# Late Q pairs evacuated two PSUM banks at a time, five of them behind the kv sum: one change to a hand-ordered attention and MLP kernel

## The chip, the cores and the metric

The kernel runs on one core of one Trainium2 chip, in one launch. The metric is the device time of that launch in microseconds; the time before is the median of three runs. A core has TensorE (PE, matmuls), VectorE (DVE), ScalarE (ACT), GpSimd (POOL) and SyncE (SP), here used to issue DMAs. Matmuls write PSUM, eight banks of 512 fp32 values in each of 128 partitions; ACT and DVE read them out ("evacuate").

## The reference

One token block of S = 2048 tokens and D = 448 goes through a linear-attention layer and a gated MLP, each behind a LayerNorm and with a residual:

```python
h  = x + A(layernorm(x))
h2 = h + B(layernorm(h))

def A(x):                                    # 16 heads of 28
    q, k, v = split(x @ wqkv)
    phi = lambda t: where(t > 0, t + 1, exp(t)) + 1e-6
    kv  = sum over s of phi(k)[s, d] * v[s, e]      # per head
    z   = sum over s of phi(k)
    o   = (phi(q) @ kv) / (phi(q) @ z + 1e-6)
    return o @ wo

def B(x):                                    # 448 -> 1792 -> 448
    return (gelu(x @ w_gate) * (x @ w_up)) @ w_down
```

All inputs and the output are bf16. The sum kv over all 2048 tokens has to be complete before any o can be formed.

## The kernel before, in words

Tokens are cut into 16 tiles of 128. Each step is a named task on one engine. A task graph (`_Graph`) derives the waits from the buffers that a task reads and writes, PSUM banks among them; the sequence on each engine is not found at run time but written out, as five strings in `ORDERS` (PE, ACT, DVE, POOL, SP). An engine runs its string strictly in order, so a task that waits holds all that stand behind it on that engine.

Names, with a tile number t, a group number q or a task number v behind them:

- Front LayerNorm, for each tile: bnst, bnag (DVE, statistics, L467 and L468), ln, rstd (ACT), negm (POOL), norm (DVE for the first four tiles, L491, else POOL, L492). Tiles 0 to 3 are transposed on TensorE (tr, L500) and copied out by ev: ev0 and ev1 on DVE (L530), ev2 and ev3 on ACT (L532). Tiles 4 to 15 get a small copy dup (ACT, L534) and a DMA transpose xT, issued on SP.
- K and V, for each tile (`kv_tile`): k and v (PE) are two halves that write the same two banks, one for K and one for V; ek = exp of K (ACT, L570), cl = clamp (POOL, L571), ph = phi(K) in SBUF (DVE, L573), evv = V to SBUF (ACT, L575). Four small accumulations in two tasks, acc..a and acc..b, add phi(K)^T V to banks 6 and 7.
- Q (`q_pair`): four token chunks of 512 with two pairs each, so eight pairs n = 2c + h, in tasks qa and qb (qa00, qb00 to qa31, qb31); a pair fills two banks with two groups of 112 rows. Pairs 0 to 3 lie between the K and V tiles (`EVENTS`), pairs 4 to 7 behind them. For pairs 0 to 3 each group is evacuated by eq (exp, L618), cq (clamp on POOL, L619) and pq (max and add on DVE straight from PSUM, L620). For pairs 4 to 7 (`SPLIT`) it is eq (exp into its final place, L626), rq (a plain copy of q into the free buffer `xn`, L627), cq (clamp in place on POOL, L628) and pq (max and add on DVE, all operands in SBUF, L629), so that both PSUM reads are ACT's.
- Behind the kv sum: kz1, kz2 (DVE, masks of the sum), then for tiles 0 and 1 nd (numerator and denominator, PE), rd and om (reciprocal and product on DVE, L656 and L657), tro (transpose, PE), evo (ACT), wo (PE), hr (residual, DVE, L662), hbnst and hbnag, hln and hrstd (ACT), normh and wrap (DVE), trh (transpose, PE), evh (copy: evh0 on ACT, evh1 on DVE). Later tiles go in pairs: nd..a and nd..b, a DMA transpose oT, wo..a and wo..b, then the second LayerNorm on POOL and a DMA transpose hT.
- MLP: gu (gate and up, PE), ge (gelu, ACT, L832), hm (product, DVE, L834), down (PE), out (residual, DVE, L758). gu0 to gu6 cover tiles 0 and 1. Task v uses gate bank `BK_G[v % 2]` and up bank `BK_U[v % 2]`.

Two halves of a product (qa and qb, k and v, acc..a and acc..b, nd..a and nd..b, wo..a and wo..b) use the two 64-row halves of TensorE on two banks crosswise: what the upper rows write in the first half, the lower rows write in the second. The graph therefore makes the second half wait for the end of the first. The tables `KV_BANKS` and `Q_BANKS` say which two of the banks 0 to 5 a tile or a pair uses, and with that which evacuation it waits for.

The two tasks nd0 and nd1, tro, trh, most of wo0 and wo1, and the last down tasks use all 128 rows of TensorE; all else uses 64.

Of the kernel before, what the change touches and what calls it, by code (L numbers as in the profile page):

```python
# [7 lines left out]
ALU = mybir.AluOpType  # L8
# [206 lines left out]
def _c_act(n):  # L215
    return 0.05 + n / 1200.0


def _c_dve(n, rate=1.0):
# [6 lines left out]
    ("q", 2), ("kv", 10), ("kv", 11), ("kv", 12), ("q", 3), ("kv", 13), ("kv", 14), ("kv", 15),  # L226
)
KV_BANKS = ((3, 2), (4, 5), (2, 0), (1, 3), (0, 2), (3, 1), (5, 4), (1, 3), (4, 5), (2, 0), (5, 4), (0, 2), (3, 1), (2, 0), (1, 3), (4, 5))
Q_BANKS = ((5, 4), (2, 0), (3, 1), (4, 5), (0, 1), (2, 3), (0, 1), (2, 3))


def bass_sequential_preLN__linear_attn_block__glu_gated_geglu__prompt_kernel(
# [16 lines left out]
    STAT_GROUPS = [[0], [1], [2], [3]] + [[t, t + 1] for t in range(4, T, 2)]  # L249
    N_DVE_NORM = cfg.get("n_dve_norm", 4)  # L250
# [6 lines left out]
    SPLIT = cfg.get("split", (4, 5, 6, 7))  # L257
# [3 lines left out]
    with es:  # L261
# [81 lines left out]
        def bank(*b):  # L343
            return [b_ps[x] for x in b]
# [4 lines left out]
        BK_G, BK_U = (0, 1), (6, 7)  # L349
# [19 lines left out]
        def op(eng, fn, r, w, name, dur, key=None, after=()):  # L369
            if key is None:  # L370
                ik[0] += 0.01
                key = ik[0]
            return G.add(eng, fn, r=r, w=w, name=name, dur=dur, key=key, after=after)
# [134 lines left out]
        first = []  # L508

        for ts in STAT_GROUPS:  # L510
            kln = 1.0 + 1.4 * ts[0] - (30.0 if ts[0] < 2 else 0.0)
            for t in ts:
                first.append(ln_stats(t, x_sb[:, t, :], b_x[t], st1, mv1, b_st1, b_mv1, kln, after=first[-1:] if t < 3 else ()))
# [3 lines left out]
            for t in ts:  # L517
                dve = t < N_DVE_NORM
                nrm = op("dve" if dve else "pool", norm(t, xn[:, t, 0:D], x_sb, mv1, rs1, None if dve else nm1), [b_x[t], b_mv1[t], b_rs1[t]] + ([] if dve else [b_nm1[t]]), [b_xn[t]], "norm%d" % t, 0.31 if dve else 0.69, kln)
                if t == 1:  # L520
                    first.append(nrm)
                tok = slice(t * 128, (t + 1) * 128)
                ktr = 4.0 + 1.6 * t
                if t < N_PE_TR:
# [4 lines left out]
                    if t < 2:  # L529
                        op("dve", lambda e, xv_=xv_, tv=tv: e.tensor_copy(xv_, tv), bank(*pb), [b_xnT[t]], "ev%d" % t, 0.33, ktr)  # L530
                    else:
                        op("act", lambda e, xv_=xv_, tv=tv: e.activation(xv_, tv, AF.Identity), bank(*pb), [b_xnT[t]], "ev%d" % t, _c_act(512), ktr)  # L532
# [382 lines left out]
```

## Time and profile before

| what | us |
|---|---|
| median of three runs (198.08 to 198.22) | 198.17 |
| profiled execution | 197.88 |
| its span, first to last instruction | 196.1 |
| TensorE busy | 191.2 |
| VectorE busy | 118.8 |
| ScalarE busy | 76.7 |
| GpSimd busy | 49.1 |

Times in the rows are microseconds from the start of the span. A timeline row has start, length, engine, line, operation, output<-inputs, shape and count; in brackets stands the idle time just before it and what ended it. Matmuls are pipelined: their rows overlap, so that TensorE's pace is read from the distance of two starts. In a row of a group, the number behind the bar is busy time, then the mean ns of one instruction, then the idle time before and its releasers. Many matmuls share the line of a helper (L435) and are told apart by their tiles and shapes: wkv_sb is K and V, wq_sb is Q, v,pk the accumulation, kvz,pqT nd, wo_sb wo, wgu_sb gu, wd_sb down.

### The profile page before, as it was taken

The numbers are of one execution on the slowest core, as the hardware profiler recorded it, in microseconds if no ns is written. First come the engines' busy times: TensorE is split into PE (matmuls) and PEld (weight loads), VectorE is DVE, ScalarE is ACT, GpSimd is POOL, SyncE is SP. The second block draws the span as 40 slices with busy tenths as digits, with TensorE's granted clock in tenths as the row PEclk, the third lists the DMA queues.
The fourth block names the chain that finished last, engine by engine and source line by source line (L and its number), as shares of the span: only waits on it lengthen the run. The fifth ranks groups of instructions, "written<-read, shape, count | busy, mean of one in ns | idle before, by whom it ended". The sixth has DMA issues, their size and how long they took to land.

```text
span 196.1 us, 5375 instructions
## 1 busy us (share of the span) xinstructions
PE 191.2 (98%) x2192; PEld 131.1 (67%) x2192; DVE 118.8 (61%) x303; ACT 76.7 (39%) x211; POOL 49.1 (25%) x100
## 2 busy tenths in 40 slices
PE   7999999999999999999999999999999999999994
PEld 7555557654489774975555656788887666679554
DVE  3999746548899974952975870972665544241512
ACT  3489865766884210330342440241234444211100
POOL 4089964533332060400220310130310000000000
PEclk9999999999999999999999999999999999999999
DMA  6985656992764318043142035134060000010111
GB/s 193 376 252 97 83 103 168 241 241 55 139 233 89 62 30 142 28 92 61 47 96 54 2 76 74 36 67 94 3 129 14 3 0 0 3 47 3 47 47 47
DMA packets 37256, 17.53 MB, mean 89 GB/s; under 512 B 28272, under 2 KB 36336, under 8 KB 37232
## 3 DMA queue, kind: packets, MB, share of 16 engines
q1 hardware_dynamic: 36352, 16.45, 36.6%
q10 hardware_dynamic: 880, 0.75, 1.2%
q8 instruction: 17, 0.28, 0.6%
q14 instruction: 7, 0.06, 0.1%
HBM read 8.72 MB, written 1.84 MB: 54 GB/s over the span
## 4 chain that ended last, share of the span: by engine, by line
PE 87%; DVE 7%; DMA 4%; issue 1%; ACT 0%; SPq 0%; DVEq 0%
PE ps L435 80%; PE ps L782 5%; DMA oT<-o_sb 2%; DVE st L467 2%; DMA x_sb<-in_A_x_dram 2%; DVE o_sb L657 1%; DVE xn L491 1%; DVE x_sb L662 1%; DVE hh L834 0%; DVE rd L656 0%; DVE hn L491 0%; DVE mv L468 0%; DVE xnT L530 0%; DVE pqT L629 0%; PE ps L674 0%
## 5 line engine op out<-in xcount | busy, mean ns | idle before, releaser
L435 PE MATMUL ps<-hnT,wgu_sb 64*128 64x512 bf16 (+1 forms) x980 | 90.6, 333 | 0.0
L435 PEld LDWEIGHTS ps<-hnT,wgu_sb 64*128 64x128 bf16 x980 | 63.0, 94 | 20.9 <-DVE hh L834 3.8
L832 ACT ACTIVATE gl<-ps 128x256 bf16<-128x256 f32 x112 | 37.0, 381 | 90.0 <-PE ps L435 62.8
L834 DVE TENSOR_TENSOR hh<-ps,gl 128x256 bf16<-128x256 f32 x112 | 42.4, 415 | 33.3 <-ACT gl L832 33.2
L435 PE MATMUL ps<-wd_sb,hh 64*128 64x448 bf16 x336 | 34.9, 349 | 0.0
L435 PEld LDWEIGHTS ps<-wd_sb,hh 64*128 64x128 bf16 x336 | 22.8, 94 | 8.9 <-DVE x_sb L758 0.2
L435 PE MATMUL ps<-wkv_sb,xnT 64*128 64x448 bf16 x192 | 23.3, 350 | 0.1
L758 DVE TENSOR_TENSOR x_sb<-ps,x_sb 128x448 bf16<-128x448 f32 (+1 forms) x17 | 9.8, 593 | 21.3 <-PE ps L435 13.9
L467 DVE BATCH_NORM_STATS2 st<-x_sb 128x6 f32<-128x448 bf16 x32 | 18.8, 616 | 2.6 <-DMA x_sb<-in_A_x_dram 2.5
L479 POOL TENSOR_SCALAR ln<-mv 128x2 f32<-128x2 f32 x7 | 1.9, 272 | 57.1 <-DVE mv L468 57.0
L573 DVE SCALAR_TENSOR_TENSOR pk<-ps,tm 128x448 bf16<-128x448 f32 x16 | 9.9, 619 | 9.2 <-PE ps L435 5.7
L435 PE MATMUL ps<-xnT,wq_sb 64*128 64x512 bf16 x112 | 15.2, 377 | 0.1
L435 PEld LDWEIGHTS ps<-wkv_sb,xnT 64*128 64x128 bf16 x192 | 9.2, 94 | 7.0 <-PE ps L435 0.5
L435 PE MATMUL ps<-wo_sb,oT 64*128 64x448 bf16 x98 | 12.6, 350 | 0.4 <-DMA oT<-o_sb 0.3
L571 POOL TENSOR_SCALAR tm<-e 128x448 bf16<-128x448 bf16 x16 | 9.0, 560 | 13.2 <-ACT e L570 12.9
L570 ACT ACTIVATE e<-ps 128x448 bf16<-128x448 f32 x16 | 8.7, 543 | 6.0 <-PE ps L435 3.8
L782 PE MATMUL ps<-wd_sb,hh 128*128 128x448 bf16 (+1 forms) x70 | 10.8, 315 | 0.0
L492 POOL TENSOR_SCALAR hn<-x_sb,nm,rs 128x448 bf16<-128x448 bf16 x14 | 10.5, 756 | 0.8 <-POOL rs L481 0.2
L662 DVE TENSOR_TENSOR x_sb<-ps,x_sb 128x448 bf16<-128x448 f32 x16 | 9.5, 618 | 1.3 <-PE ps L435 1.2
L782 PEld LDWEIGHTS ps<-wd_sb,hh 128*128 128x128 bf16 x70 | 6.7, 98 | 4.3 <-DVE x_sb L758 0.4
L657 DVE TENSOR_TENSOR o_sb<-ps,rd 128x448 bf16<-128x448 f32 x16 | 9.5, 612 | 0.1
L435 PEld LDWEIGHTS ps<-xnT,wq_sb 64*128 64x128 bf16 x112 | 6.0, 94 | 4.5 <-PE ps L435 0.6
(70 smaller groups left out, 151.2 us busy)
## 6 DMA issues: line engine op xcount, KB each, us to landing
out_dram<-x_sb SPq DMA_DIRECT2D x15, 112.0 KB, 1.7
wgu_sb<-in_B_w_gate_dram SPq DMA_DIRECT2D x7, 224.0 KB, 5.2
wgu_sb<-in_B_w_up_dram SPq DMA_DIRECT2D x7, 224.0 KB, 5.5
wd_sb<-in_B_w_down_dram SPq DMA_DIRECT2D x1, 1568.0 KB, 7.7
x_sb<-in_A_x_dram SPq DMA_DIRECT2D x2, 448.0 KB, 5.5
wkv_sb<-in_A_wqkv_dram ACTq DMA_DIRECT2D x2, 336.0 KB, 3.8
x_sb<-in_A_x_dram SPq DMA_DIRECT2D x3, 224.0 KB, 4.3
wo_sb<-in_A_wo_dram SPq DMA_DIRECT2D x2, 336.0 KB, 6.3
```

The lines of the kernel that those rows point to most:

```text
L435: ins = e.matmul(o_, l_, r_, start=s_, stop=p_, **kw)
L467: op("dve", lambda e: e.bn_stats(st[:, t, :], src_ap), [b_src], [b_st[t]], "%sbnst%d" % ("" if mv is mv1 else "h", t), 0.53, key, after=after)
L492: return lambda e: e.tensor_scalar(dst, src[:, t, :], nm[:, t:t + 1], rs[:, t:t + 1], ALU.add, ALU.mult)
L570: act_exp(lambda e: e.activation(e1[:, ie, :], oK, AF.Exp), bank(bk), [b_e1[ie]], "ek%d" % t, _c_act(D), kk)
L571: op("pool", lambda e: e.tensor_scalar(tm1[:, ie, :], e1[:, ie, :], 1.0 + EPS, 0.0, ALU.min, ALU.max), [b_e1[ie]], [b_tm1[ie]], "cl%d" % t ...
L573: op("dve", lambda e: e.scalar_tensor_tensor(pk[:, i, :, 0:GW], psK3, EPS, tm1[:, ie, :].rearrange("p (g e) -> p g e", g=NG), ALU.max, ALU ...
L657: op("dve", lambda e: e.tensor_tensor(o_sb[:, so, oc:oc + D].rearrange("p (a e) -> p a e", e=28), nd3[:, :, 0:28], rd[:, i, :].unsqueeze(2 ...
L662: op("dve", lambda e: e.tensor_tensor(h_sb[:, u, :], ps[:, b, 0:D], x_sb[:, u, :], ALU.add), bank(b) + [b_x[u]], [b_h[u]], "hr%d" % u, 0.5 ...
L758: op("dve", lambda e: e.tensor_tensor(x_sb[:, t, c0:c1], ps[:, bk, c0:c1], h_sb[:, t, c0:c1], ALU.add), bank(bk) + [b_h[t]], [bo], "out%d% ...
L782: ins = e.matmul(ps[:, bk, c0:c1], hh[:, j, hsl(t)], wd_sb[:, j, c0:c1], start=(j == 0), stop=(j == NJ - 1))
L832: G.add("act", lambda e, gi=gi, cs_=cs_, psG=psG: e.activation(gl[:, gi, cs_], psG[:, cs_], AF.Gelu_apprx_tanh), r=bank(BK_G[i]), w=[b_glh ...
L834: op("dve", lambda e, dst=dst, srcU=srcU, srcL=srcL: e.tensor_tensor(dst, srcU, srcL, ALU.mult), bank(BK_U[i]) + [b_glh], [b_ar[j_][t % HR ...
```

## The change

- Late pairs are evacuated two banks at once: eq is one exp of 112x1024, rq one Relu of 112x1024 into `xn`, cq one POOL instruction on 112x1024 (min with 1, plus 1e-6), pq one plain add on DVE of two bf16 tensors in SBUF, 112x1024. The two banks must be neighbours, in ascending order.
- Pair 3 (qa11, qb11) leaves the K and V loop: five pairs are late now. `EVENTS`, `KV_BANKS` and `Q_BANKS` change with it.
- gu tasks: even ones in banks 6 and 7, odd ones in banks 0 and 1 (before: 0 and 6, 1 and 7).
- ev0 and ev1 go from DVE to ACT. An order that was forced among the first statistics (`first`) is dropped.
- All five strings of `ORDERS` are written anew. What the prediction speaks of, for PE: v3 stands between qa00 and qb00; k13, k14, k15 stand close together; behind the sum come qa11, qb11; gu1 stands ahead of gu0, with nd4a and nd4b apart. On DVE hm7_1 goes behind om7. From wo4a on PE's sequence is nearly the old one.

```diff
 ORDERS = (
 ...
-    " acc13b qa20 acc13a acc14a qb20 acc14b acc15b acc15a qa21 nd1 nd0 qb21 qa30 nd2a tro0 nd2b tro1 wo0 wo1 qb30 qa31"
-    " qb31 trh0 trh1 wo2a wo2b gu0 gu1 nd4a nd4b gu2 gu3 gu4 gu5 wo4a wo4b gu6 nd6a gu7 nd6b down0a gu8 down0b wo6a"
+    "warm1 warm0 tr0 tr1 k0 v0 tr2 k1 tr3 v1 acc0a k2 k3 v2 qa00 v3 acc0b qb00 acc1b k4 acc1a acc2a v4 k5 acc2b acc3b"
+    " v5 acc3a k6 qa01 v6 acc4a qb01 k7 acc4b acc5b v7 k8 acc5a acc6a v8 k9 acc6b acc7b k10 v9 qa10 v10 qb10 k11 acc7a"
+    " acc8a v11 k12 acc8b acc9b v12 acc9a acc10a k13 k14 v13 k15 v14 acc10b acc11b v15 acc11a acc12a acc12b acc13b"
+    " qa20 acc13a acc14a qb20 acc14b acc15b acc15a qa11 nd1 nd0 qb11 qa30 nd2a tro1 nd2b qb30 qa21 tro0 qb21 wo0 wo1"
+    " qa31 wo2a qb31 trh0 trh1 wo2b gu1 nd4a gu0 nd4b gu3 gu2 gu5 gu4 wo4a wo4b gu6 nd6a gu7 nd6b down0a gu8 down0b"
+    " wo6a wo6b gu9 nd8a gu10 nd8b gu11 gu12 gu13 down2a wo8a down2b wo8b gu15 nd10a gu14 nd10b gu17 gu16 gu19 gu18"
 ...
-    " evv11 ek12 eq6 evv12 eq7 ek13 evv13 ek14 evv14 ek15 evv15 eq9 eq8 rq9 rq8 eq11 eq10 evo0 evo1 rq10 rq11 eq12"
-    " hln0 hrstd0 hln1 hrstd1 eq13 eq15 rq12 rq13 evh0 eq14 tbl2 ge0_0 rq14 ge0_1 ge1_0 ge1_1 rq15 ge2_0 ge2_1 ge3_0"
+    "dwk dwv dwk_t tbl ln0 rstd0 ln1 rstd1 ev0 ev1 ln2 rstd2 ln3 rstd3 ek0 ev2 ln4 rstd4 evv0 ev3 dup4 ek1 ln10"
+    " rstd10 dup5 evv1 ln6 rstd6 dup11 ek2 evv2 dup7 ek3 dup6 evv3 eq1 eq0 ln8 dup10 ek4 rstd8 evv4 ln12 rstd12 evv5"
+    " ek5 dup8 ln14 dup9 rstd14 ek6 dup12 evv6 eq3 eq2 ek7 dup13 evv7 ek8 evv8 dup15 dup14 ek9 evv9 ek10 evv10 eq5 eq4"
+    " evv11 ek11 ek12 evv12 ek13 evv13 ek14 evv14 evv15 ek15 eq8 rq8 eq6 rq6 evo1 rq12 evo0 eq10 rq10 eq12 hln0 hrstd0"
+    " hln1 hrstd1 evh0 eq14 tbl2 ge1_0 ge1_1 rq14 ge0_0 ge0_1 ge3_0 ge3_1 ge2_1 ge2_0 ge5_0 ge5_1 ge4_0 ge4_1 ge6_1"
 ...
-    " ph12 pq6 pq7 ph13 ph14 ph15 kz1 kz2 rd1 rd0 om1 om0 pq8 rd2 rd3 om2 om3 hr0 hbnst0 hr1 hbnag0 hbnst1 hbnag1"
-    " normh0 wrap0 normh1 wrap1 evh1 pq10 hr2 hbnst2 hr3 hbnag2 hbnst3 hm0_0 hm0_1 hbnag3 hm1_0 rd5 hm1_1 om5 rd4 om4"
-    " hm2_0 hm2_1 pq13 wrap3 hm3_0 hm3_1 pq14 pq9 wrap2 hm4_1 hm4_0 pq15 hm5_0 hm5_1 hr5 hr4 hbnst4 hbnst5 hbnag4"
-    " hm6_0 hbnag5 pq12 rd6 om6 rd7 hm6_1 pq11 hm7_0 hm7_1 om7 wrap4 wrap5 hm8_0 hm8_1 out1 out0 hr6 hr7 hbnst6 hbnst7"
+    " ph14 ph15 kz1 kz2 rd1 rd0 om1 om0 pq8 rd3 om3 rd2 pq6 om2 hr0 hbnst0 hr1 hbnag0 hbnst1 hbnag1 normh0 wrap0"
+    " normh1 wrap1 pq12 evh1 hr2 hr3 hbnst2 hbnst3 hbnag2 hbnag3 hm1_0 hm1_1 rd4 hm0_0 hm0_1 om4 rd5 om5 hm3_1 hm3_0"
+    " hm2_1 wrap2 hm2_0 pq10 pq14 wrap3 hm5_1 hm5_0 hm4_0 hm4_1 hr5 hr4 hbnst5 hbnst4 hm6_1 hbnag4 hbnag5 hm6_0 rd7"
+    " rd6 om6 hm7_0 om7 wrap4 wrap5 hm7_1 hm8_1 hm8_0 out0 out1 hr7 hr6 hbnst7 hbnst6 hbnag6 hm9_1 hbnag7 hm9_0 rd9"
 ...
 )
 EVENTS = (
     ("kv", 0), ("kv", 1), ("kv", 2), ("kv", 3), ("q", 0), ("kv", 4), ("kv", 5), ("kv", 6), ("q", 1), ("kv", 7), ("kv", 8), ("kv", 9),
-    ("q", 2), ("kv", 10), ("kv", 11), ("kv", 12), ("q", 3), ("kv", 13), ("kv", 14), ("kv", 15),
+    ("kv", 10), ("q", 2), ("kv", 11), ("kv", 12), ("kv", 13), ("kv", 14), ("kv", 15),
 )
-KV_BANKS = ((3, 2), (4, 5), (2, 0), (1, 3), (0, 2), (3, 1), (5, 4), (1, 3), (4, 5), (2, 0), (5, 4), (0, 2), (3, 1), (2, 0), (1, 3), (4, 5))
-Q_BANKS = ((5, 4), (2, 0), (3, 1), (4, 5), (0, 1), (2, 3), (0, 1), (2, 3))
+KV_BANKS = ((3, 2), (4, 5), (2, 0), (1, 3), (0, 2), (3, 1), (5, 4), (1, 3), (4, 5), (2, 0), (3, 1), (0, 2), (1, 3), (5, 4), (2, 0), (3, 1))
+Q_BANKS = ((5, 4), (2, 0), (5, 4), (2, 3), (0, 1), (2, 3), (0, 1), (2, 3))
+    EV_DVE = cfg.get("ev_dve", ())
-    SPLIT = cfg.get("split", (4, 5, 6, 7))
+    SPLIT = cfg.get("split", (3, 4, 5, 6, 7))
-        BK_G, BK_U = (0, 1), (6, 7)
+        BK_G, BK_U = (6, 0), (7, 1)
-                    if t < 2:
+                    if t in EV_DVE:
                         op("dve", lambda e, xv_=xv_, tv=tv: e.tensor_copy(xv_, tv), bank(*pb), [b_xnT[t]], "ev%d" % t, 0.33, ktr)
+            if n_ in SPLIT:
+                q = c * NG + g0
+                pq_ = pqT[0:GW, g0:g0 + 2, tok]
+                b_pq = [b_pqT[g0][c], b_pqT[g0 + 1][c]]
+                qs = xn[0:GW, q:q + 2, :]
+                b_qs = b_xn[q:q + 2] + b_xnd[q:q + 2]
+                psQ = ps[0:GW, p_:p_ + 2, :]
+                assert q_ == p_ + 1
+                act_exp(lambda e: e.activation(pq_, psQ, AF.Exp), bank(p_, q_), b_pq, "eq%d" % q, _c_act(2 * QCH), kq)
+                op("act", lambda e: e.activation(qs, psQ, AF.Relu), bank(p_, q_), b_qs, "rq%d" % q, _c_act(2 * QCH), kq)
+                op("pool", lambda e: e.tensor_scalar(pq_, pq_, 1.0, EPS, ALU.min, ALU.add), b_pq, b_pq, "cq%d" % q, 1.08, 60.0 + q)
+                op("dve", lambda e: e.tensor_tensor(pq_, qs, pq_, ALU.add), b_qs + b_pq, b_pq, "pq%d" % q, _c_dve(2 * QCH, 2.0), 60.0 + q)
+                return
             for n in range(2):
```

More of the change, by code (lines that the diff above doesn't have):

```diff
@@ L507, in bass_sequential_preLN__linear_attn_block__glu_gated_geglu__prompt_kernel @@
         xts = chain["sp"][-1:]
-        first = []
         for ts in STAT_GROUPS:
@@ L512, in bass_sequential_preLN__linear_attn_block__glu_gated_geglu__prompt_kernel @@
             for t in ts:
-                first.append(ln_stats(t, x_sb[:, t, :], b_x[t], st1, mv1, b_st1, b_mv1, kln, after=first[-1:] if t < 3 else ()))
+                ln_stats(t, x_sb[:, t, :], b_x[t], st1, mv1, b_st1, b_mv1, kln)
             if ts[0] >= N_DVE_NORM:
@@ L518, in bass_sequential_preLN__linear_attn_block__glu_gated_geglu__prompt_kernel @@
                 dve = t < N_DVE_NORM
-                nrm = op("dve" if dve else "pool", norm(t, xn[:, t, 0:D], x_sb, mv1, rs1, None if dve else nm1), [b_x[t], b_mv1[t], b_rs1[t]] + ([] if dve else [b_nm1[t]]), [b_xn[t]], "norm%d" % t, 0.31 if dve else 0.69, kln)
-                if t == 1:
-                    first.append(nrm)
+                op("dve" if dve else "pool", norm(t, xn[:, t, 0:D], x_sb, mv1, rs1, None if dve else nm1), [b_x[t], b_mv1[t], b_rs1[t]] + ([] if dve else [b_nm1[t]]), [b_xn[t]], "norm%d" % t, 0.31 if dve else 0.69, kln)
                 tok = slice(t * 128, (t + 1) * 128)
@@ L616, in q_pair @@
                 psQ = ps[0:GW, banks[n], :]
-                if n_ not in SPLIT:
-                    act_exp(lambda e, i=i, psQ=psQ: e.activation(e2[:, i, :], psQ, AF.Exp), bank(banks[n]), [b_e2[i]], "eq%d" % q, _c_act(QCH), kq)
-                    op("pool", lambda e, i=i: e.tensor_scalar(tm2[:, i, :], e2[:, i, :], 1.0 + EPS, 0.0, ALU.min, ALU.max), [b_e2[i]], [b_tm2[i]], "cq%d" % q, 0.58, kq)
-                    op("dve", lambda e, i=i, g=g, psQ=psQ: e.scalar_tensor_tensor(pqT[0:GW, g, tok], psQ, EPS, tm2[:, i, :], ALU.max, ALU.add),
-                       bank(banks[n]) + [b_tm2[i]], [b_pqT[g][c]], "pq%d" % q, _c_dve(QCH), kq)
-                else:
-                    sl = q % 16
-                    pq_ = pqT[0:GW, g, tok]
-                    qs = xn[0:GW, sl, :]
-                    act_exp(lambda e, pq_=pq_, psQ=psQ: e.activation(pq_, psQ, AF.Exp), bank(banks[n]), [b_pqT[g][c]], "eq%d" % q, _c_act(QCH), kq)
-                    op("act", lambda e, qs=qs, psQ=psQ: e.activation(qs, psQ, AF.Identity), bank(banks[n]), [b_xn[sl], b_xnd[sl]], "rq%d" % q, _c_act(QCH), kq)
-                    op("pool", lambda e, pq_=pq_: e.tensor_scalar(pq_, pq_, 1.0 + EPS, 0.0, ALU.min, ALU.max), [b_pqT[g][c]], [b_pqT[g][c]], "cq%d" % q, 0.58, 60.0 + q)
-                    op("dve", lambda e, pq_=pq_, qs=qs: e.scalar_tensor_tensor(pq_, qs, EPS, pq_, ALU.max, ALU.add),
-                       [b_xn[sl], b_pqT[g][c]], [b_pqT[g][c]], "pq%d" % q, _c_dve(QCH), 60.0 + q)
+                act_exp(lambda e, i=i, psQ=psQ: e.activation(e2[:, i, :], psQ, AF.Exp), bank(banks[n]), [b_e2[i]], "eq%d" % q, _c_act(QCH), kq)
+                op("pool", lambda e, i=i: e.tensor_scalar(tm2[:, i, :], e2[:, i, :], 1.0 + EPS, 0.0, ALU.min, ALU.max), [b_e2[i]], [b_tm2[i]], "cq%d" % q, 0.58, kq)
+                op("dve", lambda e, i=i, g=g, psQ=psQ: e.scalar_tensor_tensor(pqT[0:GW, g, tok], psQ, EPS, tm2[:, i, :], ALU.max, ALU.add),
+                   bank(banks[n]) + [b_tm2[i]], [b_pqT[g][c]], "pq%d" % q, _c_dve(QCH), kq)
         for kind, n in EVENTS:
```

70 rows, old and new, of the table ORDERS are left out of this document.

## The prediction

> **What bounds the kernel now.** I read the page first (busy shares, then the chain), then TensorE's timeline, then the other engines' timelines at each place where TensorE is late.
>
> ```profile
> span 196.1 us, 5375 instructions
> PE 191.2 (98%) x2192; PEld 131.1 (67%) x2192; DVE 118.8 (61%) x303; ACT 76.7 (39%) x211; POOL 49.1 (25%) x100
> PE 87%; DVE 7%; DMA 4%; issue 1%; ACT 0%; SPq 0%; DVEq 0%
> ```
>
> TensorE is busy for 98% and is 87% of the chain. The change keeps all its matmuls, so it can only win or lose where TensorE waits. The busy time hides small waits, since matmuls overlap; starts show them. A pace first: how far apart do starts lie where nothing waits?
>
> ```profile
> 20.10 1.03 PE L435 MATMUL ps<-xnT,wq_sb 64*128 64x512 bf16 x8
> 20.96 0.73 PE L435 MATMUL ps<-wkv_sb,xnT 64*128 64x448 bf16 x6
> 21.53 0.27 PE L435 MATMUL ps<-v,pk 64*128 64x113 bf16 x4
> 21.63 0.81 PE L435 MATMUL ps<-xnT,wq_sb 64*128 64x512 bf16 x6
> 22.28 0.73 PE L435 MATMUL ps<-wkv_sb,xnT 64*128 64x448 bf16 x6
> ```
>
> A Q pair costs 0.86 + 0.65 = 1.51 us, six 448-wide matmuls 0.57 (so eight 0.76, fourteen 1.33), an accumulation 0.10. Against that pace the timeline shows excess in four places: the first tiles, the first Q pair, the stretch between kv sum and first gate/up task, and two spots behind it. These decide.
>
> **The change part by part. (1) Start.** ev0 and ev1 go from DVE to ACT, and DVE's statistics are reordered.
>
> ```profile
> 7.26 0.41 DVE L530 COPY xnT<-ps 128x512 bf16<-128x512 bf16 x1
> 7.79 0.29 ACT L472 ACTIVATE ln<-mv,eps_t 128x1 f32<-128x1 f32 x1 [1.83 <-DVE mv L468]
> 10.88 0.58 ACT L532 ACTIVATE xnT<-ps 128x512 bf16<-128x512 bf16 x1
> 11.34 0.91 PE L435 MATMUL ps<-wkv_sb,xnT 64*128 64x448 bf16 x6
> 13.99 1.21 PE L435 MATMUL ps<-xnT,wq_sb 64*128 64x512 bf16 x8
> 16.10 0.74 PE L435 MATMUL ps<-wkv_sb,xnT 64*128 64x448 bf16 x6
> ```
>
> DVE sheds two copies of 0.41 and norm3 comes earlier; ACT has 1.83 us idle there to take two of 0.58, which hides them. But k2's second matmul writes bank 0, which ev3 must have read: ev3 ends at 11.46. Ahead of it ACT does the same ek0, ev2, evv0, ln4, rstd4 in another order, and ek0 waits for v0, which isn't earlier. So k2 stays at 11.3 to 11.5 and the DVE gain is lost: 0, at best 0.5. Then qa00 to k4 is 2.11 us for 1.51 + 0.2 of work: 0.4 of waiting, because a second half (b) waits for its first half (a, the other row group on the same banks), and only two accumulations lie between. The new order puts v3 there. **I take -0.35** (ends -0.85 and +0.1). k4's transpose is ready for it: dup4 moves ahead of ek1.
>
> **(2) Kv loop with one Q pair less.** Its 1.51 us move behind the kv sum. What is queued: its exps leave the middle of the ek/evv stream on ACT, its clamps POOL's, its two STT DVE's; it issues no DMA. New waits could come from banks, reused sooner without the pair between, and from dup8, now behind ek5 on ACT, so that xT8 leaves later and comes nearer to k8 (by how much isn't worked out here; it is in the upper end).
>
> ```profile
> 37.20 0.74 PE L435 MATMUL ps<-wkv_sb,xnT 64*128 64x448 bf16 x6
> 37.98 0.54 ACT L570 ACTIVATE e<-ps 128x448 bf16<-128x448 f32 x1 [0.57 <-PE ps L435]
> 39.30 0.63 DVE L573 SCALAR_TENSOR_TENSOR pk<-ps,tm 128x448 bf16<-128x448 f32 x1 [0.78 <-POOL tm L571]
> ```
>
> v14 issues until 37.77 and ph14 frees its K bank at 39.93: 2.16 us. The new gaps between a tile's v and the next user's second matmul are k11 2.08 (qa10, v10, qb10), k12 2.17, k14 2.48, k15 2.28: short by 0.1 at two. qa20's second matmul needs evv15. ACT does ek14, evv14, evv15 (0.54 each, overlapping a little) from 0.21 behind v14 on, done at about 1.7; on TensorE two accumulations, v15 and four accumulations fill 1.17: 0.5 of waiting. The old end of the loop has as much: from v14 at 37.20 to the first late Q matmul at 42.40 (quoted below) lie 5.20 us for v14, k15, v15, qa20, qb20 and nine accumulations, 0.57 + 0.76 + 0.57 + 1.51 + 0.90 = 4.31: 0.9 of waiting, at acc12a, between qa20 and qb20 and at acc15b. **I take 0** (ends -0.4 and +0.6).
>
> **(3) From kv sum to first gate/up task.**
>
> ```profile
> 42.40 1.02 PE L435 MATMUL ps<-xnT,wq_sb 64*128 64x512 bf16 x8
> 43.94 1.68 PE L435 MATMUL ps<-xnT,wq_sb 64*128 64x512 bf16 x14
> 45.46 0.37 PE L435 MATMUL ps<-kvz,pqT 64*128 64x116 bf16 x8
> 45.77 0.40 PE L683 MATMUL ps<-ident,o_sb 128*128 128x128 bf16 x4
> 46.85 0.74 PE L690 MATMUL ps<-wo_sb,oT 128*128 128x448 bf16 x3
> 44.80 1.08 ACT L626 ACTIVATE pqT<-ps 112x512 bf16<-112x512 f32 x2 [0.73 <-PE ps L435]
> 47.93 0.63 DVE L662 TENSOR_TENSOR x_sb<-ps,x_sb 128x448 bf16<-128x448 f32 x1
> 51.64 0.18 DVE L697 COPY hn<-hn 128x64 bf16<-128x64 bf16 x1
> 52.48 0.62 DVE L711 COPY hnT<-ps 128x896 bf16<-128x896 bf16 x1 [0.66 <-PE ps L704]
> 53.99 3.23 PE L435 MATMUL ps<-hnT,wgu_sb 64*128 64x256 bf16 x56
> ```
>
> The first late Q matmul to gu0 takes 53.99 - 42.40 = 11.59 us. Prices of the wide forms, which before doesn't show:
>
> ```profile
> L626 ACT ACTIVATE pqT<-ps 112x512 bf16<-112x512 f32 x8 | 4.5, 597 | 3.0 <-PE ps L435 3.0
> L832 ACT ACTIVATE gl<-ps 128x256 bf16<-128x256 f32 x112 | 37.0, 381 | 90.0 <-PE ps L435 62.8 <-DVE x_sb L662 15.6 <-DVE hn L751 4.6
> L628 POOL TENSOR_SCALAR pqT<-pqT 112x512 bf16<-112x512 bf16 x8 | 5.1, 648 | 9.0 <-ACT pqT L626 9.0
> L629 DVE SCALAR_TENSOR_TENSOR pqT<-xn,pqT 112x512 bf16<-112x512 bf16 x8 | 5.6, 712 | 0.0
> L751 DVE COPY hn<-hn 128x448 bf16<-128x448 bf16 x14 | 3.5, 274 | 1.6 <-POOL hn L492 1.6
> L491 DVE TENSOR_SCALAR xn<-x_sb,mv,rs 128x448 bf16<-128x448 bf16 x4 | 1.6, 411 | 0.4 <-ACT rs L474 0.4
> ```
>
> ACT, 1024 wide: 256 more elements cost 597 - 381 = 216 ns, so 597 + 432 = 1.03 us, against 1.08 for two narrow ones in a row: nothing gained. Relu is taken as dear as the Identity that it replaces. POOL: 0.65 to 1.30, I take 1.1. DVE's add lies between a copy's rate (274 ns for 448, 180 for the 64 of the row at 51.64: 0.24 ns an element and 0.17 us fixed, so 0.41 us) and two STT, 1.42; I take 0.73, by L491 (411 for 448; less 0.17 that is 0.54 ns an element), the row in the middle: one stream and two scalars, where the add has two streams and no scalar. By the Trainium skill's "VectorE: DVE Perf Modes", its perf-mode tier table, a bf16 tensor_tensor in SBUF goes at 2 elements a cycle; an estimate from that page is 0.69 us, which leaves the sum as it is, and no run here shows it yet.
>
> Walk with t = 0 at qa11's first matmul. kz1, nd1, nd0, qb11 come as kz1, nd1, nd0, qb21 did: qb11 at 1.54, its end 2.19, eq6 0.21 later at 2.4 (44.80 stands that far behind qb21's end). ACT then runs eq6, rq6, evo1, rq12 without a hole, 3 x 1.03 + 0.6 less overlap, to 5.8. TensorE does qa30, nd2a, tro1, nd2b, qb30, qa21 and reaches tro0 at 5.5; evo0 follows it, 5.9 to 6.5; wo0 starts at 6.6 (before: 4.45). wo1 ends at 8.2; qa31 needs banks 2 and 3 from eq10 and rq10, done at 8.6: a new wait of 0.45, with wo2a, qb31, trh0 queued behind it, hidden since hr0 to wrap1 on DVE (47.93 to 51.82, 3.9 us) brings trh1 only at 11.65 (hr0 itself is taken 1.08 behind wo0's start, as before, at 7.7). evh0 no longer stands behind eq13, eq15, rq12, rq13 on ACT; on DVE pq12 (0.73) and evh1 (0.62) follow wrap1 and end at 13.0, so the first gate/up task starts at 13.05. Less the 1.51 that moved in, that is 11.54: the filler is bought, but the chain through evo0 is late by nearly as much. **I take -0.05** (ends -0.7 and +0.6, the latter with an add of 1.42 ahead of evh1). The exchange of banks gains nothing by itself: every gate/up task needs evh0 and evh1 anyway.
>
> One rule speaks against the change. nd2a to tro0 takes 0.31 us; eight such matmuls should take 0.20, by the 0.10 of a four-matmul accumulation: 0.1 for going from 64-row to 128-row matmuls. The new order goes there twelve times instead of ten, 0.2 us, already in the walk. The Trainium skill's "TensorEngine Tiling (Array Packing)", Key Properties, says the same: changing the tiling mode drains TensorE; the trace agrees.
>
> **(4) Behind it.**
>
> ```profile
> 57.06 0.82 PE L435 MATMUL ps<-kvz,pqT 64*128 64x116 bf16 x16
> 57.71 6.28 PE L435 MATMUL ps<-hnT,wgu_sb 64*128 64x256 bf16 x112
> 75.68 0.35 PE L435 MATMUL ps<-wo_sb,oT 64*128 64x448 bf16 x1
> 76.28 1.72 PE L435 MATMUL ps<-wo_sb,oT 64*128 64x448 bf16 x13 [0.25 <-DMA oT<-o_sb]
> 77.84 1.69 PE L435 MATMUL ps<-hnT,wgu_sb 64*128 64x256 bf16 x28
> 72.25 3.90 DMA oT<-o_sb
> ```
>
> nd4a and nd4b stand side by side: 0.65 for 0.41. The new order has gu0 between: **-0.23**. wo6 takes 2.16 for 1.33; about 0.25 is a half behind its half, which stays, and 0.58 is oT7's DMA, issued at 72.25 because om7 stood behind hbnst4/5, two STT (pq12, pq11) and hm7_1. The STT are gone from there, hm7_1 goes behind om7: oT7 is issued about 2 us earlier. **-0.58** (end 0, if another transfer takes the place). What is late next there is wo6a's bank pair, free long before.
>
> The sum: -0.35 + 0 - 0.05 - 0.23 - 0.58 = -1.2 us. The profiled execution took 197.88 us, 1.78 outside its span; the median of the three runs is 198.17, and the difference is put on the median: **197.0 us**.
>
> **The rivals.** *Chain eats it:* evo0 behind rq12, and qa31 behind rq10, cost more than walked (a POOL clamp of 1.3 or an add of 1.42 ahead of om2 and evh1, +0.6, with k8 or qa20 late, +0.4): 198.17 - 1.2 + 1.0 = 198.0. For it: the walk has ACT without a hole for 6 us. Against: ACT is busy for 39% of the span, so it catches up behind. *Slower, bank reuse in the kv loop:* ACT takes evv ahead of ek for some tiles (0.54 us each), and if that lies ahead of the K bank's release at k11, k12, k14 and k15, each of them waits 0.54 more: +2.2, so 199.2. It decides from a release 2.2 us after v on, which is where the old loop stands (2.16); against it, order is planned with ek first for most. *More than forecast:* norm3's 0.5 isn't lost and the stretch after the kv sum closes up by another 0.5: 196.0. *Not what it says:* if Relu isn't among ACT's loaded functions, each turn costs a table load, 1.283 us in the row of L421, ten of them on the chain of part 3: above 203. The Trainium skill's "ScalarE: Activation LUTs", Table sets, has relu in every set; no run here shows it yet.
>
> ```profile
> L421 ACT ACT_TABLE_LOAD x1 | 1.3, 1283 | 2.4 <-issue 2.4
> ```
>
> **How the numbers follow.** Forecast (196.5 to 197.7) 0.52, chain 0.21, more 0.16, slower 0.10, table loads 0.01. A measurement tells 0.2% (0.4 us) from no change: faster is forecast, more, and a small part of the chain's, 0.72; same 0.15; slower 0.13. The range leaves out half of more and most of slower: 195.8 to 198.6.
>
> **What would show it.** TensorE's gaps: qa00 to k4 near 1.75 us; first late Q matmul to first gate/up near 13; no DMA wait at wo6a; nd4a and nd4b apart; two ACT forms of 112x1024 near 1.03 and an add near 0.7. I am wrong if k10 to k15 show starts over 0.3 apart from the pace, if xT8 holds k8, if ACT_TABLE_LOAD counts more than two, or if wo0 starts more than 7 us after the first late Q matmul.

## The result and the profile after

The changed kernel takes **203.35 us** (median of six runs, 202.22 to 203.70) against 198.16 us for the one before: 1.0249 times as long, 95% interval 1.0217 to 1.0281. The prediction was 197.0 us, range 195.8 to 198.6: the sign is wrong, and the time lies outside the range. The profile of after is that of an execution of 203.70 us.

Where is the loss? First the head of the page of after, with its granted clock in 40 slices and the shares of the chain.

```profile
span 202.0 us, 5341 instructions
PE 193.9 (96%) x2192; PEld 132.7 (66%) x2192; DVE 117.8 (58%) x296; ACT 78.9 (39%) x205; POOL 60.6 (30%) x95
PEclk9999999999759999999999999999999999999999
PE 82%; DMA 6%; DVE 4%; POOL 4%; ACT 2%; issue 1%; SPq 0%; DVEq 0%; ACTq 0%
```

POOL is 11.5 us busier with five instructions fewer, it has 4% of the chain where it had none, and two slices show a lower granted clock: the 11th and 12th, 50 to 61 us. So the place is the stretch behind the kv sum. TensorE's timeline of after there:

```profile
41.01 1.02 PE L435 MATMUL ps<-xnT,wq_sb 64*128 64x512 bf16 x8
49.80 1.04 PE L435 MATMUL ps<-xnT,wq_sb 64*128 64x512 bf16 x8 [0.19 <-ACT xn L618]
53.85 1.68 PE L435 MATMUL ps<-wo_sb,oT 64*128 64x448 bf16 x8 [3.01 <-DVE st L467]
59.44 1.85 PE L435 MATMUL ps<-hnT,wgu_sb 64*128 64x256 bf16 x28
61.13 0.37 PE L435 MATMUL ps<-kvz,pqT 64*128 64x116 bf16 x8
```

From the first late Q matmul to the first gate/up task it is 59.44 - 41.01 = 18.4 us; the walk gave 13.05. TensorE stands idle for 3.01 us ahead of wo2a. The chain of waits of after tells what stands ahead of that, and the rows of the wide operations, grouped by form, tell the price:

```profile
40.66 1.03 ACT pqT L617
41.77 3.65 POOL pqT L619
45.49 3.64 POOL pqT L619
49.23 1.56 DVE pqT L620
50.78 0.53 DVE o_sb L656
51.32 0.54 DVE x_sb L661
```

```profile
L619 POOL TENSOR_SCALAR pqT<-pqT 112x1024 bf16<-112x1024 bf16 x5 | 18.2, 3631 | 5.4 <-ACT pqT L617 5.1
L617 ACT ACTIVATE pqT<-ps 112x1024 bf16<-112x1024 f32 x5 | 5.1, 1024 | 2.5 <-PE ps L435 2.5
L620 DVE TENSOR_TENSOR pqT<-xn,pqT 112x1024 bf16<-112x1024 bf16 x5 | 5.1, 1035 | 4.2 <-POOL pqT L619 4.2
```

Read the chain downwards: eq8 on ACT, cq8 on POOL, cq6 behind it on POOL, then pq6 on DVE, behind which om2 and hr0 stand in DVE's queue. A POOL clamp of 112x1024 takes **3.63 us**, where 0.65 to 1.30 was forecast. DVE takes its work in order, so hr0 comes into the chain only at 51.32, and everything up to gate/up comes after it. The profile puts the end of the 3.01 us down to DVE's statistics, behind hr0. The DMA transpose of om2's tile, which wo2a reads, ends there too: it is issued at 51.34 and lands 2.4 us later, just ahead of wo2a at 53.85. Either way it is work that stood behind pq6.

### The profile page after: what moved, and what is told of

It is laid out like the page before. It is cut to its first block, busy times and chain, and to the rows that moved or that the text cites. A ratio compares the mean times of both kernels' runs of the same rounds, so it can differ in the third digit from the quotient of the medians.

```text
span 202.0 us, 5341 instructions
## 1 busy us (share of the span) xinstructions
PE 193.9 (96%) x2192; PEld 132.7 (66%) x2192; DVE 117.8 (58%) x296; ACT 78.9 (39%) x205; POOL 60.6 (30%) x95
## 4 chain that ended last, share of the span: by engine, by line
PE 82%; DMA 6%; DVE 4%; POOL 4%; ACT 2%; issue 1%; SPq 0%; DVEq 0%; ACTq 0%
PE ps L435 76%; PE ps L781 5%; POOL pqT L619 4%; DMA xnT<-xn 2%; DMA oT<-o_sb 2%; DVE st L467 2%; DMA x_sb<-in_A_x_dram 2%; PE ps L703 1%; DVE pqT L620 1%; DVE x_sb L661 1%; ACT pqT L617 1%; ACT xnT L528 0%; ACT ln L472 0%; ACT rs L474 0%; DVE o_sb L656 0%
## 5 line engine op out<-in xcount | busy, mean ns | idle before, releaser
L435 PE MATMUL ps<-hnT,wgu_sb 64*128 64x512 bf16 (+1 forms) x980 | 92.0, 334 | 0.0
L435 PEld LDWEIGHTS ps<-hnT,wgu_sb 64*128 64x128 bf16 x980 | 63.8, 94 | 21.8 <-DVE hh L833 5.3
L435 PEld LDWEIGHTS ps<-wd_sb,hh 64*128 64x128 bf16 x336 | 24.3, 94 | 7.4
L619 POOL TENSOR_SCALAR pqT<-pqT 112x1024 bf16<-112x1024 bf16 x5 | 18.2, 3631 | 5.4 <-ACT pqT L617 5.1
L435 PE MATMUL ps<-wo_sb,oT 64*128 64x448 bf16 x98 | 14.4, 381 | 3.5 <-DVE st L467 3.0
L435 PE MATMUL ps<-xnT,wq_sb 64*128 64x512 bf16 x112 | 15.8, 390 | 0.2 <-ACT xn L618 0.2
L486 POOL TENSOR_SCALAR nm<-mv 128x2 f32<-128x2 f32 x13 | 3.0, 232 | 32.4 <-DVE mv L468 32.0
L435 PEld LDWEIGHTS ps<-wo_sb,oT 64*128 64x128 bf16 x98 | 6.5, 98 | 7.9 <-DVE st L467 3.5
L492 POOL TENSOR_SCALAR hn<-x_sb,nm,rs 128x448 bf16<-128x448 bf16 x14 | 10.0, 722 | 0.8 <-POOL rs L481 0.2
```

Source lines behind the costliest of these rows:

```text
L435: ins = e.matmul(o_, l_, r_, start=s_, stop=p_, **kw)
L492: return lambda e: e.tensor_scalar(dst, src[:, t, :], nm[:, t:t + 1], rs[:, t:t + 1], ALU.add, ALU.mult)
L619: op("pool", lambda e: e.tensor_scalar(pq_, pq_, 1.0, EPS, ALU.min, ALU.add), b_pq, b_pq, "cq%d" % q, 1.08, 60.0 + q)
```

## The experiments

Theory A: POOL is slow at (min, add), the pair of operations that the change writes in place of (min, max). Its versions: A1, a comparison together with an arithmetic operation; A2, the tiny constant 1e-6; A3, `add` as the second operation. Theory B: the width of 1024, or the two rows of `pqT`, is dear for POOL. Theory C: the new order loses the time, whatever the clamp costs. Theory D (rival C in the text of the first experiment): DVE's adds lock POOL out while they run.

**After with the old pair of operations, still 1024 wide.**

```diff
-e.tensor_scalar(pq_, pq_, 1.0, EPS, ALU.min, ALU.add)
+e.tensor_scalar(pq_, pq_, 1.0 + EPS, 0.0, ALU.min, ALU.max)
```

> The changed kernel, with the late clamp written as before (min with 1 + 1e-6, then max with 0) instead of min with 1, then plus 1e-6; still one POOL instruction of 112x1024, in place. What it leaves out: the 1e-6 for negative q. Theory A, the pair of operations min and add is what makes POOL slow (3.63 us for 1024): the clamp falls to 1.0 to 1.3 us, TensorE no longer stops for 3.0 us behind qa31, its clock stays at 1.00, and the kernel takes 197.0 to 197.8 us, as forecast plus the 0.2 to 0.5 that the start and the kv loop gave less than forecast. Rival B, the width or the two stripes 4 KB apart make it slow: the clamp stays at 3.6 us and the kernel at 202 to 204. Rival C, DVE's adds lock POOL out: the clamp stays over 2 us wherever an add runs, 199 to 202.

Measured: 198.0 us against 198.24, ratio 0.9989 (0.9976 to 1.0002). Groups and TensorE's timeline of this kernel (its last row, k10, is used further down):

```profile
L619 POOL TENSOR_SCALAR pqT<-pqT 112x1024 bf16<-112x1024 bf16 x5 | 5.2, 1039 | 10.8 <-ACT pqT L617 10.8
L620 DVE TENSOR_TENSOR pqT<-xn,pqT 112x1024 bf16<-112x1024 bf16 x5 | 3.3, 672 | 0.0
```

```profile
41.11 1.03 PE L435 MATMUL ps<-xnT,wq_sb 64*128 64x512 bf16 x8
54.08 1.71 PE L435 MATMUL ps<-hnT,wgu_sb 64*128 64x256 bf16 x28
26.49 0.74 PE L435 MATMUL ps<-wkv_sb,xnT 64*128 64x448 bf16 x6
```

The clamp falls to 1.04 us, first late Q to gate/up takes 12.97 us (the walk: 13.05), and the whole loss is gone: one pair of operations carries it. Theories B and C fall as the cause of the loss. D falls too: in after, the last clamp (59.62 to 63.24) takes 3.62 us with no add of DVE beside it.

**After with each clamp cut into two of 112x512.**

```diff
+for hb in range(2):
+    pqh = pqT[0:GW, g0 + hb, tok]
+    ... e.tensor_scalar(pqh, pqh, 1.0, EPS, ALU.min, ALU.add)
```

> The changed kernel, its late clamp cut into two POOL instructions of 112x512 with the same operations (min with 1, plus 1e-6). Theory A (the operations): each takes about half of 3.63, 1.8 to 1.9 us, the time stays at 202 to 204. Rival B (width or stripes): each takes 0.65 us as in the kernel before, the time falls to 197 to 198.5.

Measured: 203.27 us (one execution). Its group of the halves:

```profile
L621 POOL TENSOR_SCALAR pqT<-pqT 112x512 bf16<-112x512 bf16 x10 | 19.2, 1924 | 4.6 <-ACT pqT L617 3.9
```

Two times 1.92 us is no less than 3.63: the price goes by the element, and the width is not to blame.

**Before with the new pair on its eight late clamps.**

```diff
-... e.tensor_scalar(pq_, pq_, 1.0 + EPS, 0.0, ALU.min, ALU.max) ...
+... e.tensor_scalar(pq_, pq_, 1.0, EPS, ALU.min, ALU.add) ...
```

> The kernel before, with nothing changed but the operations of its eight late clamps of 112x512: min with 1, then plus 1e-6. Theory A: each goes from 0.65 to 1.8 to 1.9 us; POOL stands before pq8, pq9 and the later pairs, the chain gets 0.5 to 3 us longer, 198.7 to 201. Rival B (width): 0.65 us each and 198.2.

Measured: 199.6 us, ratio 1.0064 (1.0045 to 1.0084). Its group, the two clamps on its chain, and the wait that they bring:

```profile
L628 POOL TENSOR_SCALAR pqT<-pqT 112x512 bf16<-112x512 bf16 x8 | 15.4, 1921 | 2.9 <-ACT pqT L626 2.5
```

```profile
42.75 1.94 POOL pqT L628
44.77 1.93 POOL pqT L628
```

```profile
52.77 0.95 PE L704 MATMUL ps<-ident,hn 128*128 128x128 bf16 x14 [1.45 <-DVE hn L697]
```

The same pair of operations, three times as dear as before, costs the old kernel 0.6% and the new one 2.5%. In both, two clamps stand in a row on the chain ahead of DVE: in the old one two of 512 elements, each 1.3 us longer than before; in the new one cq8 and cq6 with 1024 each, 3.6 us apiece.

**Eleven pairs of operations on POOL alone**, 112x512 bf16, behind all of POOL's work in the kernel before (L862 to L872, one instruction each; one execution, 198.62 us).

```diff
+... e.tensor_scalar(tm2[:, 0, :], e2[:, 1, :], 1.0, EPS, ALU.min, ALU.add) ...   (and ten more)
```

> The kernel before with eleven more POOL instructions of 112x512 bf16 at the end of POOL's sequence, where it has nothing else to do; their result is used nowhere. In this order: (min 1+1e-6, max 0), (min 1, add 1e-6), (min 1, add 1), (add 1e-6, min 1), (min 1) alone, (add 1e-6) alone, (max 0, min 1), (mult 1, add 1e-6), (min 1, mult 0.5), (max 0, add 1e-6), (add 1, mult 0.5). Theory A1, a comparison with an arithmetic operation is what has no quick path: numbers 2, 3, 4, 9 and 10 take 1.92 us, the rest 0.6 to 0.7. Rival A2, the tiny constant: 2, 4, 6, 8 and 10 are slow, 3 is quick. Rival A3, add as the second operation: 2, 3, 8 and 10 are slow, 4, 9 and 11 quick. The time of the kernel stays at 198.2.

Measured, with five of the eleven rows:

```profile
L863 POOL TENSOR_SCALAR tm<-e 112x512 bf16<-112x512 bf16 x1 | 2.0, 1957 | 0.1
L864 POOL TENSOR_SCALAR tm<-e 112x512 bf16<-112x512 bf16 x1 | 1.9, 1923 | 0.1
L866 POOL TENSOR_SCALAR tm<-e 112x512 bf16<-112x512 bf16 x1 | 1.5, 1497 | 0.1
L862 POOL TENSOR_SCALAR tm<-e 112x512 bf16<-112x512 bf16 x1 | 0.7, 697 | 0.1
L869 POOL TENSOR_SCALAR tm<-e 112x512 bf16<-112x512 bf16 x1 | 0.6, 619 | 0.1
```

| operations (line) | us |
|---|---|
| min, max (L862) | 0.70 |
| mult, add (L869); add, mult (L872) | 0.62; 0.62 |
| min alone (L866); add alone (L867) | 1.50; 1.49 |
| min, add of 1e-6 (L863); of 1 (L864) | 1.96; 1.92 |
| add, min (L865); max, min (L868) | 1.94; 1.92 |
| min, mult (L870); max, add (L871) | 1.94; 1.93 |

Each was timed once. A2 falls: the constant changes nothing. A1 falls: (max, min) has no arithmetic and is slow. A3 falls as well: (mult, add) is quick, and (add, min) and (min, mult) are slow. What holds is a list: three of eleven are quick; two operations can cost less than one, and (min, max) costs little more than a third of (max, min). Why these three are quick stays open.

**After with 52 idle matmuls ahead of wo2a**, so that TensorE has work in its hole.

```diff
-" qa31 wo2a qb31 ..."
+" qa31 warm2 wo2a qb31 ..."
+    for _ in range(52): ins = e.matmul(ps[:, 0, 0:128], ones_bf[:], ones_bf[:], start=True, stop=True)
```

> The changed kernel with 52 matmuls of 128x128x128 more on TensorE between qa31 and wo2a, into bank 0, whose result nobody reads: about 2.8 us of work in the 3.0 us in which TensorE stood idle there. Theory: of the 5.2 us that the change costs, about 2.5 are the lower clock that was granted after the idle stretch (0.62 and 0.53 in 52 to 60 us); with TensorE kept at work the clock stays at 1.00 and the time falls to 200.5 to 201.3. Rival: the clock follows something else (the transposes, the narrow matmuls), the clock falls anyway and the time stays at 203 to 204.

Measured: 202.44 us, ratio 1.0202 (1.0181 to 1.0223). Stretches of 4 us, first after, then this kernel (busy us of PE, PEld, DVE, ACT, POOL; granted clock; DMA share; GB/s):

```profile
52.00:56.00 4.00, 2.15 (x12) 1.01 (x14) 2.92 (x9) 1.00 (x4) 3.92 (x2) 0.62 0.68 154
56.00:60.00 4.00, 4.00 (x32) 2.29 (x30) 1.62 (x3) 2.27 (x3) 0.92 (x2) 0.53 0.82 283
```

```profile
52.00:56.00 4.00, 3.94 (x59) 3.01 (x56) 3.50 (x10) 0.99 (x4) 3.92 (x2) 1.00 0.48 85
56.00:60.00 4.00, 3.16 (x50) 2.51 (x50) 2.82 (x6) 3.11 (x3) 2.59 (x2) 1.00 1.00 349
```

And the first gate/up task of this kernel:

```profile
58.51 1.71 PE L435 MATMUL ps<-hnT,wgu_sb 64*128 64x256 bf16 x28 [0.84 <-ACT pqT L617]
```

The clock stays at 1.00, so the lower clock came with the hole. The ratio falls from 1.0249 to 1.0202: of the 5.2 us lost, filling the hole gives back about 0.9 (by the two intervals 0.2 to 1.7), less than the 2.5 that I had expected. With the full clock TensorE waits again, 0.84 us, at gate/up: on DVE evh1 stands behind pq12, which waits for its clamp until 57.18. The evacuation is late by itself.

**Before with two pieces of the new order on TensorE alone.**

```diff
-" ... k3 v2 v3 qa00 acc0b acc1b qb00 k4 ..."
+" ... k3 v2 qa00 v3 acc0b qb00 acc1b k4 ..."
-" ... gu0 gu1 nd4a nd4b gu2 ..."
+" ... gu0 nd4a gu1 nd4b gu2 ..."
```

> The kernel before with two edits of TensorE's sequence alone: v3 and acc0b between qa00 and qb00, and gu1 between nd4a and nd4b. By terms 1 and 4 of the prediction it gains 0.2 to 0.6 us (197.6 to 198.0); rival: both waits come back right behind, at k4 (its transposed tile lands late) and at the next banks, and the time stays at 198.1 to 198.3.

Measured: 199.96 us, ratio 1.0083 (1.0065 to 1.0100), slower than the theory and the rival had it. Its waits on TensorE:

```profile
14.12 1.03 PE L435 MATMUL ps<-xnT,wq_sb 64*128 64x512 bf16 x7 [0.28 <-DVE pk L573]
20.30 0.74 PE L435 MATMUL ps<-wkv_sb,xnT 64*128 64x448 bf16 x6 [0.50 <-DVE pqT L620]
57.33 0.38 PE L435 MATMUL ps<-kvz,pqT 49*128 49x116 bf16 x7 [0.33 <-DVE x_sb L662]
78.48 1.72 PE L435 MATMUL ps<-wo_sb,oT 64*128 64x448 bf16 x13 [0.58 <-DVE x_sb L758]
```

DVE's queue kept the order that fitted the old one, and behind both moves TensorE now waits for DVE: in the first Q pair, at k6, and at nd4a. The last row is at wo6, where before waited too (0.25 us, for oT7's DMA), so it isn't the moves' alone. Terms 1 and 4 of the sum can't be had by edits of TensorE's queue alone. That the new order of the other queues is what makes them good is a reading; no run here tries it by itself.

**The first experiment with dup8 ahead of ek5 and dup9 ahead of ln14 on ACT**, so that two transposes are issued earlier.

```diff
-" ek5 dup8 ln14 dup9 rstd14 ek6 ..."
+" dup8 ek5 dup9 ln14 rstd14 ek6 ..."
```

> The changed kernel with the old clamp (min, max) and one more edit: on ACT dup8 goes ahead of ek5 and dup9 ahead of ln14, so that the transposes xT8 to xT10 are issued earlier. Theory: k10 waited 0.24 us for xT10 because dup8 stood behind ek5; the wait goes, 197.6 to 197.9. Rival: ek5 and ph5 come later by the same 0.1 to 0.25 and hold a K bank instead, 198.0 to 198.2.

Measured: 197.95 us, ratio 0.9973 (0.9960 to 0.9985). TensorE's rows for k10 and, far behind, wo12a:

```profile
26.25 0.74 PE L435 MATMUL ps<-wkv_sb,xnT 64*128 64x448 bf16 x6
119.06 0.93 PE L435 MATMUL ps<-wo_sb,oT 64*128 64x448 bf16 x7 [0.57 <-DMA oT<-o_sb]
```

k10 starts 0.24 us sooner and waits for nothing, so the wait was dup8 and dup9; in the profiled execution another transpose gives 0.57 back. The time is not told apart from the first experiment's, their intervals overlap.

**The clamp inside DVE's instruction, none on POOL** (on top of the last kernel).

```diff
-op("pool", ... e.tensor_scalar(pq_, pq_, 1.0 + EPS, 0.0, ALU.min, ALU.max) ...)
-op("dve", ... e.tensor_tensor(pq_, qs, pq_, ALU.add) ...)
+op("dve", ... e.scalar_tensor_tensor(pq_, pq_, 1.0 + EPS, qs, ALU.min, ALU.add) ...)
```

> The kernel of e6_best without any late clamp on POOL: the clamp goes into DVE's add, one scalar_tensor_tensor of 112x1024 (min with 1 + 1e-6, then plus the Relu). DVE's instruction should go from 0.68 to about 1.25 us (two of 0.69 less one fixed part), POOL's 1.04 us between exp and add go. Theory: the chain behind the kv sum isn't bound by the clamp any more once it takes 1.04 us, so the time stays within 0.3 us of e6_best (197.7 to 198.3); rival: the step less shortens the way to evh1 and the pairs behind, 197.2 to 197.6.

Measured: 199.06 us, ratio 1.0032 (1.0019 to 1.0045). DVE's timeline ahead of gate/up:

```profile
52.53 1.22 DVE L619 SCALAR_TENSOR_TENSOR pqT<-pqT,xn 112x1024 bf16<-112x1024 bf16 x1
53.67 0.62 DVE L709 COPY hnT<-ps 128x896 bf16<-128x896 bf16 x1
```

1.22 us instead of 0.68, five times, and once directly ahead of evh1: a POOL instruction fewer is paid for on DVE. The time lies above both forecasts. First late Q to gate/up takes 54.39 - 41.04 = 13.35 us, 0.38 more than without this edit; the rest of the loss lies elsewhere.

**Before with the wide evacuation alone**, in the (min, max) form, for its four late pairs; and the same with eq12 moved behind hrstd1 on ACT.

```diff
+act_exp(... e.activation(pq_, psQ, AF.Exp) ...); e.activation(qs, psQ, AF.Relu)
+e.tensor_scalar(pq_, pq_, 1.0 + EPS, 0.0, ALU.min, ALU.max); e.tensor_tensor(pq_, qs, pq_, ALU.add)
...
-" ... rq10 eq12 hln0 hrstd0 hln1 hrstd1 rq12 ..."
+" ... rq10 hln0 hrstd0 hln1 hrstd1 eq12 rq12 ..."
```

> The kernel before with the wide evacuation alone, for its four late pairs: one exp and one Relu of 112x1024, the old clamp (min, max) of 112x1024, one bf16 add; the same TensorE sequence, four late pairs, ev0 and ev1 on DVE, old banks. It leaves out the 1e-6 for negative q. By the prediction ACT and POOL gain nothing and DVE sheds 2.8 us between 53 and 72 us, so that oT7 is issued 1.5 to 2 us earlier and the wait at wo6a (0.58) goes: 197.5 to 197.8. Rival: the wide exp and Relu hold both banks longer, qa31 and gu0 start later by 0.3 to 0.6, and the time stays at 198.0 to 198.4.

> The kernel of e8_old_wide with one move on ACT: the wide eq12 behind hln0 to hrstd1 instead of ahead of them. In e8_old_wide TensorE waited 0.84 us for the second LayerNorm of tiles 0 and 1 since eq12 (1.02 us) stood ahead of hln0. Theory: that wait goes and the gain at wo6a (0.58) stays, 197.4 to 197.9 where the kernel before has 198.2 to 198.5. Rival: rq12 and evh0 come later by the same 0.5 and hold gu0, 198.0 to 198.4.

Measured: 198.34 us, ratio 0.9988 (0.9977 to 1.0000), then 197.83 us, ratio 0.9969 (0.9958 to 0.9981). TensorE at trh0, and what stands ahead of hln0 on ACT, in the first of the two; then trh0 and wo6 in the second:

```profile
52.11 1.08 PE L708 MATMUL ps<-ident,hn 128*128 128x128 bf16 x14 [0.84 <-DVE hn L701]
49.56 1.02 ACT L621 ACTIVATE pqT<-ps 112x1024 bf16<-112x1024 f32 x1 [1.19 <-PE ps L435]
```

```profile
51.22 1.26 PE L708 MATMUL ps<-ident,hn 128*128 128x128 bf16 x14
76.13 1.73 PE L435 MATMUL ps<-wo_sb,oT 64*128 64x448 bf16 x14
77.70 0.49 PE L435 MATMUL ps<-hnT,wgu_sb 64*128 64x256 bf16 x6
```

A wide exp of 1.02 us ahead of the layer norm's statistics costs 0.84 us at trh0; moved behind them it costs nothing there, and wo6 no longer waits for oT7. The first of the two has the time of its rival, but not for the rival's reason. The wide evacuation with a quick clamp and that one move gives 0.3%, as much as the whole change with it and with dup8 and dup9 moved (0.9973): the other parts bring nothing that these runs tell apart.

## Why the prediction was wrong, step by step

**The step that failed** is in part 3: "POOL: 0.65 to 1.30, I take 1.1." The row behind it was of (min, max); the change writes (min, add), a pair that no POOL instruction of before uses. I bounded the size of the operation and not its kind. It measured 3.63 us, 2.8 times the upper end, with +5.3 us on the stretch (18.43 against 11.59 + 1.51). No rival had it. "Chain eats it" had the right place, a POOL clamp ahead of DVE's om2, at 1.3 us; "slower" had a wrong mechanism: at k11 to k15 the profile lists no wait of TensorE, where 0.54 each was feared.

The rest, read where the clamp is quick (the first experiment):

- **Part 1**, -0.35 forecast, -0.17 found, and not in the way that was forecast. TensorE's row of qb00 in before; then, in after, those of k2 and k4, and the piece of the chain ahead of k4:

```profile
15.26 0.82 PE L435 MATMUL ps<-xnT,wq_sb 64*128 64x512 bf16 x6
```

```profile
10.91 0.95 PE L435 MATMUL ps<-wkv_sb,xnT 64*128 64x448 bf16 x6
15.92 0.74 PE L435 MATMUL ps<-wkv_sb,xnT 64*128 64x448 bf16 x6 [0.26 <-DMA xnT<-xn]
```

```profile
11.36 4.42 DMA xnT<-xn
```

  k2 starts at 10.91 (at 11.07 in the first experiment), not at 11.3 to 11.5: the start gains the 0.3 to 0.4 us that I had called lost. But k4 then waits for xT4, whose transpose takes 4.42 us from its issue, and I had called it ready: what the start and v3's new place gain ahead of k4 is cut to 0.17 there. The reading of before was off as well. Of its 0.4 us of waiting only 0.2 lie between qa00 and qb00 (15.26 - 13.99 = 1.27 for 0.86 + 0.20), where a half waits for its half; the other 0.2 lie ahead of k4 (0.84 for 0.65), whose transpose was issued at 12.92 and took 3.1 us.
- **Part 2**, 0 forecast, +0.39 found: 41.11 against 42.40 - 1.51 - 0.17. Of this, 0.24 is k10's wait for xT10. The mechanism stood at the upper end (dup8 behind ek5, a transpose late); the tile was another.
- **Part 3** with a quick clamp: 12.97 against the walk's 13.05. Its parts hold too: wo0 6.61 us behind the first late Q matmul (6.6), wide ACT 1.02 (1.03), the add 0.67 (0.73). The estimate of 0.69 that the prediction drew from the Trainium skill's "VectorE: DVE Perf Modes", perf-mode tier table, agrees with the 0.67.
- **Part 4**: nd4a and nd4b stand apart without the 0.23. wo6a has lost its DMA wait, as two rows of after show, 1.57 us apart instead of 2.16:

```profile
81.30 1.73 PE L435 MATMUL ps<-wo_sb,oT 64*128 64x448 bf16 x14
82.87 1.36 PE L435 MATMUL ps<-hnT,wgu_sb 64*128 64x256 bf16 x22
```

  But of those 0.81 us TensorE waits 0.54 more at other places behind gate/up, 0.17 of it at gu5 and 0.10 at wo4a. That these are the new order's doing was not tried.
- **Table loads**: two, as before. Relu costs none, as the Trainium skill's "ScalarE: Activation LUTs", Table sets, has it.

Term by term, the two profiled executions differ by -0.17 + 0.39 - 0.13 - 0.27 = -0.2 us, and their medians, 198.0 and 198.24, by as much. So with a quick clamp the forecast of 197.0 would still have been 1 us too low, though 198.0 lies inside its range: I gave every removed wait its full length, 1.16 us in all (0.35, 0.23 and 0.58), and parts 1 and 4 brought 0.44. More than half was taken by what was late next.

## What to carry to other kernels

Price an instruction by its engine, its shape **and its operations**: a row with another pair of operations bounds nothing, and a range for a form that was never seen must be as wide as the dearest form of that engine. On an engine that feeds an in-order queue, ask what stands behind it: the same pair of operations cost the old kernel 0.6% and the new one, with clamps twice as wide, 2.5%. When queues were planned together, moving one of them alone can bring the waits back elsewhere.

## What was not expected of the hardware

- POOL's tensor_scalar of 112x512 bf16 takes from 0.62 to 1.96 us with its pair of operations, and a single operation takes 1.5 us, more than twice the quick pairs.
- DVE's add of two bf16 tensors takes 0.69 us alone and 1.56 us beside POOL's slow clamp. Both rows are of after, with POOL's four clamps in a row beside them:

```profile
41.77 14.77 POOL L619 TENSOR_SCALAR pqT<-pqT 112x1024 bf16<-112x1024 bf16 x4 [2.04 <-ACT pqT L617]
45.52 1.56 DVE L620 TENSOR_TENSOR pqT<-xn,pqT 112x1024 bf16<-112x1024 bf16 x1 [1.60 <-POOL pqT L619]
56.57 0.69 DVE L620 TENSOR_TENSOR pqT<-xn,pqT 112x1024 bf16<-112x1024 bf16 x1 [1.44 <-POOL pqT L619]
```

  The Trainium skill's "SBUF — State Buffer", Summary: rules for kernel authors, says that of a DVE instruction with two SBUF inputs and a GpSimd one that reads SBUF the second to issue is fully blocked until the first ends. The contention agrees; the full block does not: the add of 45.52 ends at 47.08, two microseconds ahead of the clamp that began just before it (45.49 to 49.13).
- With a hole of 3.01 us on TensorE (50.84 to 53.85) the granted clock is 0.62 from 52 to 56 us and 0.53 from 56 to 60; with 52 idle matmuls in the hole it stays at 1.00, and a hole of 1.45 us (before with the new pair on its clamps) leaves the mean clock at 1.000.
